# A gate-and-up feed-forward block: all weights of F tiles 0 to 3 are loaded before the transposed x, and eight groups run on 256 tokens first

## The chip, the cores and the metric

The kernel runs on one core of a Trainium2 chip. The metric is the device time of one execution in microseconds, as the median of several runs. Engines are named as in the profile: PE is TensorE (PEld its weight loads), DVE is VectorE, ACT is ScalarE, POOL is GpSimd, SP is SyncE.

## What is computed

```python
B, S, D, F = 1, 2048, 512, 1376        # all bfloat16

def reference(x, w_gate, w_up, w_down):
    g = _silu(x @ w_gate)
    u = x @ w_up
    return (g * u) @ w_down
```

## The kernel before

All of the schedule is written out by hand: each engine has its own list of instructions in program order, and semaphores join the lists. Nothing is reordered by a scheduler.

**Tiles.** Tokens (S = 2048) are cut into four chunks of 512. F = 1376 is cut into ten tiles of 128 and a rest of 96. D = 512 is the contraction of the first two products, in four steps `dk` of 128. A *group* is one PSUM bank: for one chunk and one F tile there is a gate group (G) and an up group (U). Each group is made by four `dk` steps, and each step by two matmuls with 64 weight columns each that run side by side on the two column halves of the array (`gu_step`, L332 to L351). ACT applies silu to the gate bank (L291), DVE multiplies it with the up bank into `hT_sb` (L305). There are eight banks, used in turn; a group may start when the readers of the group eight places before it are done (`free`, L327). Groups of type X and Y do the rest of F. After all four chunks the product with `w_down` follows (L428, L451, L503), and results are copied out and stored.

**Order of groups in a chunk.** G0 U0, G1 U1, then G2 G3 U2 U3, then G4 U4 up to G9 U9, then X (L232).

**The start.** The first matmuls need x transposed (D on partitions). For the first 256 tokens of chunk 0, x is loaded as it lies (`xn_sb`, one load named xn) and transposed on TensorE (L369, L377); DVE and ACT copy the four results to `xT_sb` (L309, L291). All other tokens come by transposing loads: x0b (tokens 256 to 383), x0c (384 to 511), and x1, x2, x3 (512 tokens each). Before xn has landed, TensorE runs matmuls on constants: `N_WARM` of width 512 and `N_FILL` of width 128 (L357 to L362).

**The loads.** Weights of gate and up come in four slabs of F tiles, 0 to 1, 2 to 3, 4 to 6 and 7 to 10, each slab as one gate load (wg0, wg2, wg4, wg7) and one up load (wu0, wu2, wu4, wu7); the last 32 columns of `w_up` have a load of their own (wut), which only the X groups need. ACT issues wg0 (L111); SyncE issues everything else in this order: xn, wu0, x0b, x0c, wg2, wu2, wg4, wu4, wg7, wu7, wut, x1, x2, x3, then the `w_down` loads (L113 to L132). Each load has its own semaphore; `need(name)` makes TensorE wait for it once.

**The first groups.** As only 256 tokens of chunk 0 are there at first, G0, G1, U0 and U1 run on those first (G0 and G1 alternating over `dk`), and then on the other 256 tokens, with G0's first piece cut in two, so that x0b and x0c are waited for one after the other:

```python
            g0, u0, g1, u1 = groups[NT:NT + 4]
            for dk in range(KD):
                for g in (g0, g1):
                    gu_step(g, dk, 0, HT)
            for g in (u0, u1):
                gu_matmuls(g, 0, HT)
            gu_matmuls(g0, HT, HT + P)
            gu_matmuls(g0, HT + P, SC)
            for g in (u0, g1, u1):
                gu_matmuls(g, HT, SC)
```

(HT is 256, P 128, SC 512.) All other groups, from G2 on, run on 512 tokens at once.

Of the kernel before, what the change touches and what calls it, by code (L numbers as in the profile page):

```python
# [6 lines left out]
BF16 = mybir.dt.bfloat16  # L7
FP32 = mybir.dt.float32

N_WARM = 6  # L10
N_FILL = 2


def bass_standalone__swiglu_ffn__prompt_kernel(nc, x, w_gate, w_up, w_down, out):
    _, S, D = x.shape
    F = w_gate.shape[1]
    P = 128
# [13 lines left out]
    HC = P // 2  # L31
    NXN = HT // P
    NB = 8
# [8 lines left out]
    UPH = F + 32  # L42
# [4 lines left out]
    with ExitStack() as es:  # L47
# [19 lines left out]
        banks = [psum[:, i, :] for i in range(NB)]  # L67
# [15 lines left out]
        def load_sem(name):  # L83
            loads[name] = sem(f"s_{name}")
            return loads[name]

        ones_w = nc.const_aps.tensor(1.0, [P, P], BF16)
        ones_m = nc.const_aps.tensor(1.0, [P, SC], BF16)
# [3 lines left out]
        def load_x(eng, name, t0, t1):  # L92
            eng.dma_start_transpose(
                xT_sb[:, :, t0:t1], xf[t0:t1, :]
            ).then_inc(load_sem(name), 16)

        def load_w(eng, name, src, base, f0, f1):
            eng.dma_start(
                w_sb[:, :, base + f0:base + f1],
                src[:, f0:f1].rearrange("(k p) f -> p k f", p=P),  # L100
            ).then_inc(load_sem(name), 16)

        slabs = [(0, 2), (2, 4), (4, 7), (7, NFT)]
        slab_of = {ft: a for a, b in slabs for ft in range(a, b)}

        def load_slab(eng, a, b):
            load_w(eng, f"wg{a}", w_gate, 0, a * P, min(b * P, F))
            load_w(eng, f"wu{a}", w_up, UPH, a * P, min(b * P, F - 32))

        def loads_on_scalar(act):  # L110
            load_w(act, "wg0", w_gate, 0, 0, slabs[0][1] * P)  # L111

        def loads_on_sync(sp):  # L113
            sp.dma_start(
                xn_sb[:, :, :].rearrange("p j d -> p (j d)"), xf[0:HT, :].rearrange("(p j) d -> p (j d)", j=NXN)
            ).then_inc(load_sem("xn"), 16)
            load_w(sp, "wu0", w_up, UPH, 0, slabs[0][1] * P)
            load_x(sp, "x0b", HT, HT + P)
            load_x(sp, "x0c", HT + P, SC)
            for a, b in slabs[1:]:  # L120
                load_slab(sp, a, b)
            load_w(sp, "wut", w_up, F - (F - 32), F - 32, F)
            for c in range(1, NSC):
                load_x(sp, f"x{c}", c * SC, (c + 1) * SC)
            sp.dma_start(
                wd_sb[:, 0:NFF, :], w_down[0:NFF * P, :].rearrange("(k p) d -> p k d", p=P)
            ).then_inc(load_sem("wd"), 16)
            for c in range(NSC):
                sp.dma_start(
                    wdt_sb[R * c:R * (c + 1), :, :], w_down[NFF * P:F, :].rearrange("(q p) d -> p q d", p=R)  # L130
                ).then_inc(load_sem(f"wdt{c}"), 16)
            sp.dma_start(wdl_sb[:, :], w_down[NFF * P:F, LASTA:D]).then_inc(load_sem("wdl"), 16)  # L132
# [3 lines left out]
        groups = []  # L136
# [3 lines left out]
        def add_group(kind, **what):  # L140
            g = dict(kind=kind, at=len(groups), bank=banks[turn[(len(groups) - KD) % NB]], readers=[], **what)
            groups.append(g)
            return g
# [75 lines left out]
        for dk in range(KD):  # L219
            g = add_group("T", dk=dk)  # L220
# [8 lines left out]
        NT = len(groups)  # L229
# [11 lines left out]
        for at in range(NST):  # L241
# [4 lines left out]
            for c0, c1 in [(0, LASTA), (LASTA, LASTB), (LASTB, D)] if end else [(0, D)]:  # L246
                g = add_group("O", t=t, c0=c0, c1=c1, c=c)
# [3 lines left out]
                    eng, g, kind="copy", out=o_sb[ob][:, c0:c1], src=g["bank"][:, 0:c1 - c0],  # L251
# [6 lines left out]
        def rows_of(t):  # L258
            if t < NXN:
                return of[0:HT, :].rearrange("(p j) d -> j p d", j=NXN)[t]  # L260
            return of[t * P:(t + 1) * P, :]
# [14 lines left out]
            ).then_inc(s_I, 1)  # L276

        def on_scalar(act):
            loads_on_scalar(act)
            act.activation(adummy[:, 0:4], zero_c, ACT.Silu)  # L280
            for op in act_ops:
                act.wait_ge(s_P, op["g"]["at"] + 1)
                if op["kind"] == "silu":
                    if op["free"]:
                        act.wait_ge(s_D, op["free"])
                    fn = ACT.Silu
                else:
                    if op["stored"][1]:
                        act.wait_ge(*op["stored"])
                    fn = ACT.Copy  # L290
                act.activation(op["out"], op["src"], fn).then_inc(s_A, 1)  # L291
            for t, c0, c1, ob, eng, n in stores:
                if (c0, c1) == (0, LASTA):
                    act.wait_ge(s_A, n)
                    act.dma_start(rows_of(t)[:, c0:c1], o_sb[ob][:, c0:c1]).then_inc(s_out[ob], 16)
# [16 lines left out]
        def on_tensor(pe):  # L312
# [14 lines left out]
            def free(g):  # L327
                if g["at"] >= NT + NB:
                    for eng, n in groups[g["at"] - NB]["readers"]:
                        after(eng, n)  # L330

            def gu_step(g, dk, n0, n1):  # L332
                c, ft = g["c"], g["ft"]
                if c > 0:
                    need(f"x{c}")
                if c == 0 and n1 > HT:
                    need("x0b")
                if c == 0 and n1 > HT + P:
                    need("x0c")
                if c == 0 and n0 < HT:  # L340
                    after(*xt_ready[dk])
                need(("wg" if g["kind"] == "G" else "wu") + str(slab_of[ft]))
                col = (0 if g["kind"] == "G" else UPH) + ft * P
                for m in (0, HC):
                    ins = pe.matmul(  # L345
                        g["bank"][m:m + HC, n0:n1], lhsT=w_sb[:, dk, col + m:col + m + HC],
                        rhs=xT_sb[:, dk, c * SC + n0:c * SC + n1], start=(dk == 0), stop=(dk == KD - 1),
                        tile_position=(0, m),
                    )
                if n1 == SC and dk == KD - 1:  # L350
                    ins.then_inc(s_P, 1)  # L351

            def gu_matmuls(g, n0, n1):
                for dk in range(KD):
                    gu_step(g, dk, n0, n1)

            def warm(n, width):  # L357
                for i in range(n):
                    pe.matmul(banks[NB - 1][:, 0:width], lhsT=ones_w, rhs=ones_m[:, 0:width], start=True, stop=True)  # L359

            warm(N_WARM, SC)
            warm(N_FILL, P)  # L362
            pe.wait_ge(s_J, 1)
            need("xn")
            for dk in range(KD - 1):
# [11 lines left out]
                    ins = pe.transpose(tview_last()[m:m + HC, i, :], xn_sb[:, i, c0:c0 + HC], ident[:, :])  # L377
            ins.then_inc(s_P, 1)

            g0, u0, g1, u1 = groups[NT:NT + 4]  # L380
            for dk in range(KD):
                for g in (g0, g1):
                    gu_step(g, dk, 0, HT)
            for g in (u0, u1):
                gu_matmuls(g, 0, HT)
            gu_matmuls(g0, HT, HT + P)
            gu_matmuls(g0, HT + P, SC)
            for g in (u0, g1, u1):
                gu_matmuls(g, HT, SC)

            for g in groups[NT + 4:]:
                kind = g["kind"]
                if kind == "O":
                    break
                free(g)
                if kind in "GU":
                    gu_matmuls(g, 0, SC)
                elif kind == "X":
                    c = g["c"]
                    need(f"wg{slab_of[NFF]}")  # L400
                    need("wut")
                    for dk in range(KD):
                        for m in (0, HC):
                            ins = pe.matmul(  # L404
                                g["bank"][m:m + HC, :], lhsT=w_sb[:, dk, XC0 + m:XC0 + m + HC],
                                rhs=xT_sb[:, dk, c * SC:(c + 1) * SC],
                                start=(dk == 0), stop=(dk == KD - 1), tile_position=(0, m),
                            )
                    ins.then_inc(s_P, 1)
                elif kind == "Y":  # L410
                    need(f"wu{slab_of[NFF]}")
                    for dk in range(KD):
                        for c in (2 * g["pi"], 2 * g["pi"] + 1):
                            y0, y1 = yblk(c)
                            ins = pe.matmul(  # L415
                                g["bank"][y0:y1, :], lhsT=w_sb[:, dk, YC0:YC0 + 64],
                                rhs=xT_sb[:, dk, c * SC:(c + 1) * SC],
                                start=(dk == 0), stop=(dk == KD - 1),
                                tile_position=(0, y0), skip_group_check=True,
                            )  # L420
                    ins.then_inc(s_P, 1)
# [78 lines left out]
            for g in last:  # L500
# [4 lines left out]
                    start=False, stop=True, skip_group_check=True,  # L505
# [35 lines left out]
```

## Time and profile before

| | us |
|---|---|
| median of 3 runs | 119.92 (119.9 to 120.52) |
| span of the profiled execution | 118.3 |
| median minus that span | 1.62 |
| PE busy in the span | 115.6 |
| DVE busy | 43.4 |
| ACT busy | 35.5 |
| first matmul on constants | 0.77 |
| first transpose on TensorE | 3.77 |
| first matmul of a group | 4.51 |
| first matmul of an X group (end of chunk 0's other groups) | 21.82 |

For the profiled execution the span is the only time that is given; the runs of the median are other executions. Times within an execution are counted from the start of the span. Busy time of PE counts matmuls from start to a modelled end, and neighbours overlap, so that the spacing of starts tells more than the mean duration does. The time of a DMA issue is the time it holds the issuing engine's queue; its landing is counted from the start of the issue. "Wait" in the text means that an engine stands still for a semaphore.

### The profile page before, as it was taken

The page shows a single profiled execution, that of the slowest core. Times are in us where ns is not written, and L with a number is a line of the kernel's source. Part 1 is how long each engine was busy: PE and PEld are TensorE (multiplying, and loading weights), DVE is VectorE, ACT ScalarE, POOL GpSimd, SP SyncE. Part 2 cuts the span into 40 slices and gives each one's busy share as a digit, 9 for nine tenths or more (in the row PEclk, how much of TensorE's full clock was granted, in tenths as well). Part 3 has the DMA queues.
Part 4 walks back from the last instruction along what each step waited for, and adds up shares of the span by engine and source line. Part 5 has one row for each costly group of instructions (what it writes and reads, how often), then busy time and mean ns, then how long its engine had stood idle before and what let it go on. Part 6 is the DMA issues. An engine that isn't in the chain of part 4 may idle for free.

```text
span 118.3 us, 2985 instructions
## 1 busy us (share of the span) xinstructions
PE 115.6 (98%) x1342; PEld 69.8 (59%) x1342; DVE 43.4 (37%) x68; ACT 35.5 (30%) x61; POOL 0.4 (0%) x5
## 2 busy tenths in 40 slices
PE   7999999999999999999999999999999999999993
PEld 2786666666666666666666666654444444464452
DVE  0133443353433443524442534369700040214331
ACT  5244324454234364243264232370000030203001
POOL 1000000000000000000000000000000000000000
DMA  3999999990000000000000000000000032050512
GB/s 90 272 287 345 225 224 247 309 241 19 0 6 0 0 0 6 0 0 6 0 6 0 0 0 0 6 0 0 6 0 6 0 105 78 0 178 32 195 44 89
DMA packets 16540, 8.92 MB, mean 75 GB/s; under 512 B 8592, under 2 KB 16400, under 8 KB 16528
## 3 DMA queue, kind: packets, MB, share of 16 engines
q1 hardware_dynamic: 15856, 8.38, 27.3%
q10 hardware_dynamic: 672, 0.36, 1.0%
q8 instruction: 10, 0.16, 0.6%
q14 instruction: 2, 0.02, 0.0%
HBM read 4.81 MB, written 2.10 MB: 58 GB/s over the span
## 4 chain that ended last, share of the span: by engine, by line
PE 98%; DVE 0%; issue 0%
PE psum L345 59%; PE psum L451 24%; PE psum L428 7%; PE psum L404 3%; PE psum L359 2%; PE psum L415 1%; PE psum L369 0%; PE psum L377 0%; DVE o_sb L309 0%; PE psum L503 0%
## 5 line engine op out<-in xcount | busy, mean ns | idle before, releaser
L345 PE MATMUL psum<-xT_sb,w_sb 128*64 128x512 bf16 (+2 forms) x680 | 69.9, 367 | 0.0
L345 PEld LDWEIGHTS psum<-xT_sb,w_sb 128*64 128x64 bf16 x680 | 46.0, 110 | 23.0
L305 DVE TENSOR_TENSOR hT_sb<-sg_sb,psum 128x512 bf16<-128x512 f32 x40 | 27.5, 688 | 40.4 <-PE psum L345 36.6
L291 ACT ACTIVATE sg_sb<-psum 128x512 f32<-128x512 f32 x40 | 23.8, 596 | 40.5 <-PE psum L345 40.5
L451 PE MATMUL psum<-wd_sb,hT_sb 32*128 32x512 bf16 x480 | 26.9, 374 | 0.0
L451 PEld LDWEIGHTS psum<-wd_sb,hT_sb 32*128 32x128 bf16 x480 | 13.0, 93 | 13.0 <-issue 0.4
L309 DVE CAST o_sb<-psum 128x512 bf16<-128x512 f32 (+1 forms) x11 | 6.4, 603 | 25.2 <-PE psum L451 19.9
L291 ACT ACTIVATE o_sb<-psum 128x512 bf16<-128x512 f32 (+1 forms) x7 | 3.7, 580 | 33.0 <-PE psum L451 25.9
L428 PE MATMUL psum<-wd_sb,hT_sb 128*128 128x512 bf16 (+2 forms) x60 | 8.9, 308 | 0.0
L428 PEld LDWEIGHTS psum<-wd_sb,hT_sb 128*128 128x128 bf16 x60 | 4.6, 98 | 4.6 <-issue 0.4
L305 DVE TENSOR_TENSOR ht_sb<-sgy_sb,yu_sb 32x512 bf16<-32x512 f32 x8 | 5.5, 683 | 0.4
L404 PE MATMUL psum<-xT_sb,w_sb 128*64 128x512 bf16 x32 | 4.2, 379 | 0.0
L305 DVE TENSOR_TENSOR ht_sb<-sgx_sb,psum 32x512 bf16<-32x512 f32 x4 | 2.8, 692 | 3.5 <-ACT sgx_sb L291 3.5
L291 ACT ACTIVATE sgx_sb<-psum 32x512 f32<-32x512 f32 x4 | 2.3, 587 | 4.5 <-PE psum L404 4.5
L359 PE MATMUL psum<-const-bfloat16-1.0 128*128 128x512 bf16 (+1 forms) x8 | 2.9, 545 | 0.8 <-PEq L526 0.8
L451 PE MATMUL psum<-wdt_sb,ht_sb 32*128 32x512 bf16 (+1 forms) x48 | 3.3, 371 | 0.0
L404 PEld LDWEIGHTS psum<-xT_sb,w_sb 128*64 128x64 bf16 x32 | 2.2, 110 | 1.2
L359 PEld LDWEIGHTS psum<-const-bfloat16-1.0 128*128 128x128 bf16 x8 | 1.0, 136 | 2.4 <-issue 2.4
L291 ACT ACTIVATE sgy_sb<-psum 64x512 f32<-64x512 f32 x4 | 2.4, 589 | 0.1
L451 PEld LDWEIGHTS psum<-wdt_sb,ht_sb 32*128 32x128 bf16 x48 | 1.3, 93 | 1.3
L415 PE MATMUL psum<-xT_sb,w_sb 128*64 128x512 bf16 x16 | 1.9, 379 | 0.0
L280 ACT ACT_TABLE_LOAD x1 | 1.3, 1283 | 1.2 <-PEq L526 1.2
(19 smaller groups left out, 7.2 us busy)
## 6 DMA issues: line engine op xcount, KB each, us to landing
out_dram<-o_sb SPq DMA_DIRECT2D x15, 128.0 KB, 1.8
wd_sb<-in_w_down_dram SPq DMA_DIRECT2D x1, 1280.0 KB, 8.0
w_sb<-in_w_up_dram SPq DMA_DIRECT2D x2, 256.0 KB, 3.9
w_sb<-in_w_gate_dram SPq DMA_DIRECT2D x1, 480.0 KB, 6.7
w_sb<-in_w_up_dram SPq DMA_DIRECT2D x1, 448.0 KB, 7.3
w_sb<-in_w_gate_dram SPq DMA_DIRECT2D x1, 384.0 KB, 4.9
w_sb<-in_w_up_dram SPq DMA_DIRECT2D x1, 384.0 KB, 5.9
wdt_sb<-in_w_down_dram SPq DMA_DIRECT2D x4, 96.0 KB, 6.3
```

Source lines behind the costliest of these rows:

```text
L280: act.activation(adummy[:, 0:4], zero_c, ACT.Silu)
L291: act.activation(op["out"], op["src"], fn).then_inc(s_A, 1)
L305: ins = dve.tensor_tensor(op["out"], op["a"], op["b"], ALU.mult)
L309: ins = dve.tensor_copy(op["out"], op["src"])
L345: ins = pe.matmul(g["bank"][m:m + HC, n0:n1], lhsT=w_sb[:, dk, col + m:col + m + HC], rhs=xT_sb[:, dk, c * SC + n0:c * SC + n1], start=(dk ...
L359: pe.matmul(banks[NB - 1][:, 0:width], lhsT=ones_w, rhs=ones_m[:, 0:width], start=True, stop=True)
L404: ins = pe.matmul(g["bank"][m:m + HC, :], lhsT=w_sb[:, dk, XC0 + m:XC0 + m + HC], rhs=xT_sb[:, dk, c * SC:(c + 1) * SC], start=(dk == 0), ...
L415: ins = pe.matmul(g["bank"][y0:y1, :], lhsT=w_sb[:, dk, YC0:YC0 + 64], rhs=xT_sb[:, dk, c * SC:(c + 1) * SC], start=(dk == 0), stop=(dk == ...
L428: ins = pe.matmul(g["bank"][:, 0:c1 - c0], lhsT=hT_sb[:, fk, t * P:(t + 1) * P], rhs=wd_sb[:, fk, c0:c1], start=(start and fk == 0), stop= ...
L451: ins = pe.matmul(g["bank"][:, 0:c1 - c0], lhsT=h(r, g["t"]), rhs=w[R * r:R * (r + 1), c0:c1], start=(start and n == 0), stop=final, tile_ ...
```

## The change

The warm-up has five matmuls of width 512 rather than six, and the fill behind it is four pairs of matmuls of 64 rows each, one in each row half of the array and each into a bank of its own, rather than two matmuls of 128 rows. ACT issues no load any more. SyncE issues xn, wg0, wu0, wg2, wu2, wut, x0b, x0c, wg4, wu4, wg7, wu7, x1 and so on. TensorE runs the first eight groups (G0 and G1 alternating, U0, U1, G2, G3, U2, U3) on tokens 0 to 255, then G0 on tokens 256 to 383 and 384 to 511, then the other seven on tokens 256 to 511; groups from G4 on run on 512 tokens.

```diff
-N_WARM = 6
-N_FILL = 2
+N_WARM = 5
+N_FILL = 4
...
-        def loads_on_scalar(act):
-            load_w(act, "wg0", w_gate, 0, 0, slabs[0][1] * P)
-
         def loads_on_sync(sp):
             sp.dma_start(
                 xn_sb[:, :, :].rearrange("p j d -> p (j d)"), xf[0:HT, :].rearrange("(p j) d -> p (j d)", j=NXN)
             ).then_inc(load_sem("xn"), 16)
-            load_w(sp, "wu0", w_up, UPH, 0, slabs[0][1] * P)
+            for a, b in slabs[:2]:
+                load_slab(sp, a, b)
+            load_w(sp, "wut", w_up, F - (F - 32), F - 32, F)
             load_x(sp, "x0b", HT, HT + P)
             load_x(sp, "x0c", HT + P, SC)
-            for a, b in slabs[1:]:
+            for a, b in slabs[2:]:
                 load_slab(sp, a, b)
-            load_w(sp, "wut", w_up, F - (F - 32), F - 32, F)
...
         def on_scalar(act):
-            loads_on_scalar(act)
             act.activation(adummy[:, 0:4], zero_c, ACT.Silu)
...
             warm(N_WARM, SC)
-            warm(N_FILL, P)
+            for i in range(N_FILL):
+                for h in range(2):
+                    pe.matmul(
+                        banks[NB - 2 + h][:, 0:P], lhsT=ones_w[h * HC:(h + 1) * HC, :],
+                        rhs=ones_m[h * HC:(h + 1) * HC, 0:P], start=True, stop=True, tile_position=(h * HC, 0),
+                    )
...
-            g0, u0, g1, u1 = groups[NT:NT + 4]
+            first = groups[NT:NT + NB]
+            g0, u0, g1, u1 = first[:4]
             for dk in range(KD):
                 for g in (g0, g1):
                     gu_step(g, dk, 0, HT)
-            for g in (u0, u1):
+            for g in [u0, u1] + first[4:]:
                 gu_matmuls(g, 0, HT)
             gu_matmuls(g0, HT, HT + P)
             gu_matmuls(g0, HT + P, SC)
-            for g in (u0, g1, u1):
+            for g in first[1:]:
                 gu_matmuls(g, HT, SC)
 
-            for g in groups[NT + 4:]:
+            for g in groups[NT + NB:]:
```

## The prediction

> **What bounds the kernel now.** I read the page first, then the chain of work that ended last in order of time, then the start of the kernel in finer steps. The page:
>
> ```profile
> span 118.3 us, 2985 instructions
> PE 115.6 (98%) x1342; PEld 69.8 (59%) x1342; DVE 43.4 (37%) x68; ACT 35.5 (30%) x61; POOL 0.4 (0%) x5
> PE 98%; DVE 0%; issue 0%
> ```
>
> TensorE is the chain. What the chain does at the start is seen in its first pieces (start, length, what):
>
> ```profile
> 0.77 2.93 PE psum L359 x8
> 3.71 0.06 issue
> 3.77 0.51 PE psum L369 x12
> 4.27 0.31 PE psum L377 x3
> 4.58 17.44 PE psum L345 x200
> ...
> 22.88 17.27 PE psum L345 x160
> ```
>
> A full chunk of 512 tokens takes 17.27 us for 80 pairs of 64-column matmuls, 216 ns a pair. The first chunk runs from 4.51 to 21.82 us, 17.31 us, though it is cut into smaller pieces and its data arrives while it runs. So it loses at most 0.04 us, and only two things can change the time: when the first real matmul starts (4.51), and whether a load comes later than TensorE needs it. The loads are issued by SyncE thus (start, time on its queue):
>
> ```profile
> 0.74 0.40 SPq L114 DMA_DIRECT2D xn_sb<-in_x_dram  x1
> 1.20 0.41 SPq L98 DMA_DIRECT2D w_sb<-in_w_up_dram  x1
> 1.66 2.58 SPq L93 DMA_TRANSPOSE xT_sb<-in_x_dram  x2
> 4.29 0.58 SPq L98 DMA_DIRECT2D w_sb<-in_w_gate_dram  x1
> 4.92 0.50 SPq L98 DMA_DIRECT2D w_sb<-in_w_up_dram  x1
> ...
> 8.83 10.05 SPq L93 DMA_TRANSPOSE xT_sb<-in_x_dram  x3
> ```
>
> and, asked for narrow windows, the list of DMA issues gives the time to landing (last number):
>
> ```profile
> xn_sb<-in_x_dram SPq DMA_DIRECT2D x1, 256.0 KB, 2.9
> w_sb<-in_w_gate_dram ACTq DMA_DIRECT2D x1, 256.0 KB, 3.6
> w_sb<-in_w_up_dram SPq DMA_DIRECT2D x1, 256.0 KB, 4.0
> xT_sb<-in_x_dram SPq DMA_TRANSPOSE x1, 4.1
> xT_sb<-in_x_dram SPq DMA_TRANSPOSE x1, 3.2
> ```
>
> Adding issue and landing: xn 3.64, wg0 (issued on ACT at 0.75) 4.35, wu0 5.20, x0b 5.77, x0c (issued 2.98) about 6.2. Needed: xn at once, wg0 by 4.51, wu0 by 5.39, x0b by 6.26, x0c by 6.48. So x0c arrives 0.26 us early and everything is just in time. From 2.7 to 5.5 us the DMA engines are full (share 1.05 to 1.32 in the windows table); at 5.5 to 6.0 they fall to 0.73 and 89 GB/s, because SyncE spent 1.66 to 4.25 on the two transposing loads.
>
> **The change, part by part.** All times on the scale of the span.
>
> 1. Start. xn keeps its place and issue time. Its sixteen completion increments come in two halves, at 3.07 to 3.19 and at 3.45 to 3.64; the late half still has packets of about 245 ns, against 84 ns undisturbed, when wg0's first packets appear at 2.73 on engines that have finished xn. If that disturbance vanished altogether xn would land by 3.19, 0.45 earlier; if it stays, nothing changes. In the changed kernel wg0 stands behind xn in the same queue, issued at 1.20; wg2 on a drained queue took from 4.29 to 5.53, 1.24 us, to its first packet, so wg0 has packets ready at 2.44 and goes on at the same 2.73. So most of the disturbance stays: I take 0.15 earlier. The fill no longer stands in the way: five 512-wide warm-ups at 427 ns and four pairs of 107 ns end at 0.77 + 2.13 + 0.43 = 3.33 (now 3.51). If the row halves did not run as pairs it would be 3.76, a cost of about 0.1; but the transposes of L369 show pairs, two of them every 53 ns at the same cold clock.
>
> 2. wg0 from ACT to SyncE. Issue moves by 0.45 later, but each DMA engine drains xn, then wg0, then wu0 in one row (32 packets of 512 B at 27 ns, 0.86 us each load), so landing at 4.35 and 5.20 stays. Taken as 0; if the cover at 2.73 were gone it is 0.45 late. ACT loses an issue of 0.46 us ahead of a table load that ends at 2.53, long before its first copy at 4.20: 0. The Trainium skill, "DMA: Bandwidth & Descriptors", section "Issuing engines are not separate DMA queues", says that DMAs from different engines share the same 16 DMA engines and that spreading them saves only issue time. By that rule the 0.15 of step 1 would be nothing too, and the sum 0.15 larger; the packets, which drain one load after another on each engine, agree.
>
> 3. x0b and x0c move behind wg2, wu2 and wut: three loads ahead of two, on full engines. One 256 KB load behind another costs 0.85 us in the stream (wu0 behind wg0) and up to 1.13 (wg2 lands at 7.49, wu2 at 8.62). I take the first for wg2, the second for wu2: 6.05 and 7.18. wut has 32 packets of 64 B an engine at 11 ns: 0.35, so 7.53. x0b came 0.57 behind wu0 and x0c 0.45 behind x0b: 8.10 and 8.55. TensorE needs them later than before: four more half groups, each four pairs of 109 ns (0.436 us), so wg2 is due at 4.51 + 4 x 0.436 = 6.26, wu2 at 7.13, x0b at 8.00 and x0c 0.22 later, 8.22. Lateness: wg2 none, wu2 0.05, x0b 0.10, x0c 0.33. These don't add; the latest decides, so 0.35, with 0.05 by the short interval throughout (8.27) and 0.6 by the long one. What waits behind it is all of TensorE, which runs in order; ACT and VectorE have nothing to give there.
>
> 4. Smaller pieces: 16 full pairs become 32 half pairs, 32 x 109 - 16 x 216 = 0.03 us.
>
> 5. The loads behind. SyncE reaches wg4 at about 6.2 to 6.6, not 5.46 (five weight issues of 0.46 to 0.55 ahead of two transposing ones of 1.27), while the engines are still at x0b and x0c, so the dip at 5.5 to 6.0 goes. wg4 landed at 10.36 and wu4 at 11.91 and are due at 11.47 and 12.33; behind x0c at 8.55 they come one and two 384 KB loads later (1.55 between them now): 10.1 and 11.65. Cost 0, and at most 0.3 if that cover went. x1 lands at 17.0 and is due at 22.7, with over five to spare; wut is not due before 21.8. All banks are free again in time: silu 0.60 and multiply 0.69 for each gate and up pair of 0.87.
>
> Sum: -0.15 + 0.35 + 0.03 = +0.23. The profiled execution would have a span of about 118.5. The median of the runs shown is 119.92, 1.62 above the span; I carry that over unchanged: 120.2 (119.6 to 120.6 from the ends of steps 1 and 3).
>
> **The rivals.**
>
> Faster. xn lands with its first half, at 3.19: transposes start 0.4 earlier, the late half of the engines catches up, and x0c is on time. That gives -0.37, 119.55. For more, the thin covers have to count: 0.26 at x0c, 0.42 at wu4. The three runs spread over 0.62 us, which may be such waits in executions other than the profiled one; the new order removes them for wg4 and wu4. Together down to -0.9, 119.0. For it: two halves of xn's landing, and the dip at 5.5. Against: the profile shows no wait to be removed after 4.51.
>
> Slower, by a full queue. x1's issue took 5.60 us against 2.38 and 1.99 for the same load twice later; it was over at 14.43, when wu7 landed (7.11 + 7.3 = 14.4). With five weight loads outstanding the issue waits. In the changed kernel x0b is issued at about 3.6 behind wg0, wu0, wg2, wu2 and wut, also five, and x0c, wg4 and wu4 are queued behind it on SyncE. If x0b has to wait for wu0 or wg2 (5.2, 6.05), x0c's issue ends at about 7.3 to 8.2, and lands some 1.8 after, as x0c now does against its end of issue at 4.25 (6.2) with a little queue in that: 9.1 to 9.9. Late by 0.9 to 1.7, less 0.15: 120.7 to 121.5. It decides from the point where the issue of x0b takes over 2 us. Against: x0b has a quarter of x1's packets, and may fit where x1 did not.
>
> Slower, by the clock. 512-wide warm-ups are 427 ns apart, the same width later 216; the last cold spacing is at 4.32 and the first fast one at 4.51, about 3.6 us after TensorE's first matmul, so real work starts just as the clock does. The new fill ends 0.18 earlier and leaves a longer gap before the transposes. If the change of clock then came one such stretch later, 3.6 us would run at half speed: 1.8 lost, 121.7. Against: more gap is little, and the granted clock is 1.00 throughout. The Trainium skill, "TensorE: Matmul & The Clock Gate", Part 1, has such a gate with a free-running window of 3.4 us; the 3.6 us here agrees, and one trace can't show whether the window is free-running.
>
> No effect: xn and every load as now, x0c within its 8.22: +0.03, 119.95.
>
> **How the numbers follow.** A measurement of this kernel can tell about 0.5%, 0.6 us, from no change: below 119.3 counts as faster, above 120.5 as slower. Forecast 0.34, of which 0.08 above 120.5; faster rival 0.28, 0.24 of it below 119.3; queue 0.24; clock 0.06; no effect 0.08. Faster 0.24; same 0.26 + 0.04 + 0.08 = 0.38; slower 0.08 + 0.24 + 0.06 = 0.38. The range leaves out the clock (0.06), the far end of the queue (0.07) and that of the faster rival (0.04): 119.1 to 121.1. The forecast's own range is 119.6 to 120.6.
>
> **What would show it.** Step 1: start of the first transpose (3.77 now) at about 3.6; at 3.4 the faster rival. Step 2: landing of wg0 at 4.3 and wu0 at 5.2. Step 3: a gap or a longer spacing in TensorE near 8.0 to 8.6, and x0c landing at 8.3 to 8.8. Queue: SyncE's time for x0b over 2 us. Clock: 256-wide pairs of the first groups 214 ns apart instead of 109. Step 5: no wait at 11 to 13 us, and 17.27 us for each later chunk. If TensorE has no gap in the first chunk and starts as now, or the gap exceeds 1 us, my landing times are wrong.

## The result and the profile after

The changed kernel is slower: 121.25 us (median of 7, 120.77 to 122.63) against 120.12 us before (median of 7 in the same comparison), a ratio of 1.0103 with a 95% interval of 1.0075 to 1.0132. That is 0.15 outside the range that I gave (119.1 to 121.1), and on the side of the queue rival (120.7 to 121.5), not of the forecast (120.2). The ratios here and below leave out executions more than 1.5% slower than the fastest of the same kernel; the medians hold them all. The profiled execution took 122.63 us, the longest of the seven, so it shows more than the usual loss; the profile of old_fill below, a kernel with the same loads (120.91 us), is nearer to the median.

The page of the changed kernel, the lines that answer to those of before (span, engines, and the chain by engine):

```profile
span 121.2 us, 3058 instructions
PE 117.7 (97%) x1378; PEld 72.2 (60%) x1379; DVE 43.4 (36%) x68; ACT 35.4 (29%) x61; POOL 0.4 (0%) x5
PE 87%; SPq 6%; DMA 5%; issue 1%; DVE 0%
```

Before, TensorE alone was the chain (98%). Now the first 14 us of it belong to SyncE's queue and to one DMA. In order of time (start, length, what):

```profile
3.91 2.68 SPq L93
...
6.63 1.26 SPq L93
...
7.94 6.10 DMA w_sb<-in_w_gate_dram
14.04 0.14 issue
14.17 1.06 PE psum L342 x8
...
25.79 17.27 PE psum L342 x160
```

SyncE stands 2.68 us in the issue of x0b, then 1.26 in that of x0c, reaches wg4 only at 7.94 (before: 5.46), wg4 lands 6.10 later, and TensorE's first 512-wide group (G4) starts at 14.17. Before, it started at 11.47. That is 2.70 of the 2.9 us between the two spans; the wait for wu4 behind it is 0.2. Each later chunk again takes 17.27.

The chain names what came last; it does not say what the wait cost. TensorE's own lines do (in brackets the idle time before the line):

```profile
4.75 9.02 PE L342 MATMUL psum<-xT_sb,w_sb 128*64 128x256 bf16 x136
14.17 1.06 PE L342 MATMUL psum<-xT_sb,w_sb 128*64 128x512 bf16 x8 [0.41 <-DMA w_sb<-in_w_gate_dram]
```

The last pair ahead of G4 started at 13.49, so with wg4 there G4 would have started at 13.60. By this spacing TensorE stood still for 0.57 us at wg4, and for 0.17 more at wu4. The other 2.13 us of G4's delay were lost earlier in this execution: the first group started at 4.75 instead of 4.51, wu0 (landed at 6.57) cost about 0.16, and 16 pairs ran 213 ns apart instead of 109, which is about 1.7. In old_fill and no_wait_x0 below, the stops at wg4 and wu4 together come to 0.72 and 0.52 us. Before, there is no such stop. So in these three profiles the late wg4 and wu4 cost 0.5 to 0.7 us, where the medians of the same kernels lie 0.7 to 1.1 us above the kernel before.

The DMA engines in the meantime (last two columns: their share and GB/s):

```profile
7.00:8.00 1.00, 1.00 (x14) 0.85 (x12) 0.00 (x0) 0.00 (x0) 0.00 (x0) 1.00 1.00 84
8.00:9.00 1.00, 1.00 (x18) 0.94 (x16) 0.00 (x0) 0.00 (x0) 0.00 (x0) 1.00 0.85 146
9.00:10.00 1.00, 1.00 (x24) 1.00 (x22) 0.00 (x0) 0.00 (x0) 0.00 (x0) 1.00 0.59 65
```

Before they moved 294, 309 and 347 GB/s in these three microseconds. The dip that I had expected to close has become longer: no load is queued behind x0c until SyncE has issued wg4.

### The profile page after: what moved, and what is told of

Read it like the earlier page. It is cut to its first block, busy times and chain, and to the rows that moved or that the text cites. A ratio compares the mean times of both kernels' runs of the same rounds, so it can differ in the third digit from the quotient of the medians.

```text
span 121.2 us, 3058 instructions
## 1 busy us (share of the span) xinstructions
PE 117.7 (97%) x1378; PEld 72.2 (60%) x1379; DVE 43.4 (36%) x68; ACT 35.4 (29%) x61; POOL 0.4 (0%) x5
## 4 chain that ended last, share of the span: by engine, by line
PE 87%; SPq 6%; DMA 5%; issue 1%; DVE 0%
PE psum L342 52%; PE psum L454 24%; PE psum L431 7%; DMA w_sb<-in_w_gate_dram 5%; SPq L93 3%; PE psum L407 3%; SPq L98 2%; PE psum L418 1%; SPq L111 0%; DVE o_sb L306 0%; PE psum L506 0%
## 5 line engine op out<-in xcount | busy, mean ns | idle before, releaser
L342 PE MATMUL psum<-xT_sb,w_sb 128*64 128x512 bf16 (+2 forms) x712 | 72.1, 364 | 0.5 <-DMA w_sb<-in_w_gate_dram 0.4
L342 PEld LDWEIGHTS psum<-xT_sb,w_sb 128*64 128x64 bf16 x712 | 48.5, 113 | 23.4 <-ACT sg_sb L288 0.6
L306 DVE CAST o_sb<-psum 128x512 bf16<-128x512 f32 (+1 forms) x11 | 6.4, 604 | 25.2 <-PE psum L454 19.9
L356 PE MATMUL psum<-const-bfloat16-1.0 128*128 128x512 bf16 x5 | 2.3, 621 | 0.8 <-PEq L529 0.8
L407 PEld LDWEIGHTS psum<-xT_sb,w_sb 128*64 128x64 bf16 x32 | 2.3, 110 | 1.2
L306 DVE COPY xT_sb<-psum 128x256 bf16<-128x256 bf16 x2 | 0.5, 292 | 2.8 <-PE psum L371 2.8
```

The lines of the kernel that those rows point to most:

```text
L306: ins = dve.tensor_copy(op["out"], op["src"])
L342: ins = pe.matmul(g["bank"][m:m + HC, n0:n1], lhsT=w_sb[:, dk, col + m:col + m + HC], rhs=xT_sb[:, dk, c * SC + n0:c * SC + n1], start=(dk ...
L407: ins = pe.matmul(g["bank"][m:m + HC, :], lhsT=w_sb[:, dk, XC0 + m:XC0 + m + HC], rhs=xT_sb[:, dk, c * SC:(c + 1) * SC], start=(dk == 0), ...
```

## The experiments

Three theories. **W**: x0b holds SyncE, wg4 is issued late, and TensorE waits for wg4. **X**: TensorE waits for x0b and x0c (the place where prediction and queue rival had it). **Clock**: the new fill makes TensorE's clock switch later. For Clock there is something in the profile: the 256-wide pairs were 213 ns apart until 8.4 us and 109 after, while before they were 109 apart from 4.5 on. Below, the wider spacing is called half pace.

**again**: the changed kernel as it is.

> The changed kernel once more, for a second profile. Queue theory (the issue of x0b waits until loads ahead of it have landed, so x0c lands near 9.5 and TensorE waits from about 8.0): 256-wide pairs 109 ns apart from 4.5 us on, one wait of 0.9 to 1.3 us ahead of x0b and x0c, about 121.2 us. Clock theory (the shorter fill makes the clock switch one stretch later): pairs 213 ns apart until about 8.4, no wait for x0b or x0c, about 121.2 to 122.6 us. In both, SyncE's time for x0b is about 2.7 us.

121.01 us against 120.19 (23 runs of the kernel before), ratio 1.0062 (1.0033 to 1.0091). So the loss is 0.6 to 1.0%. The execution that was profiled here took 248.7 us with TensorE at half its pace from end to end, and I read no stage of TensorE from it. On SyncE's queue x0b took 1.50 us, not the 2.7 that both theories expected; wg4 was issued at 6.70 and landed at 10.45.

**old_fill**

```diff
-N_WARM = 5
-N_FILL = 4
+N_WARM = 6
+N_FILL = 2
...
-            for i in range(N_FILL):
-                for h in range(2):
-                    pe.matmul(
...
+            warm(N_FILL, P)
```

> The changed kernel with the fill of the kernel before (six warm-ups of 512, two of 128 rows by 128). Queue theory: no effect, 121.2 us and the same wait at 8 to 9.5. Clock theory: the clock switches at 4.4 in the profile and the time goes back to about 120.1.

121.18 us, 1.0096 (1.0064 to 1.0128): the old fill brings nothing back. Its chain of waits:

```profile
3.86 1.62 SPq L93
5.52 1.26 SPq L93
6.83 5.63 DMA w_sb<-in_w_gate_dram
12.60 10.71 PE psum L342 x96
```

The same links with a shorter hold: G4 starts at 12.60, 1.13 later than before, and the span is 1.3 longer (119.6). Of the 1.13, TensorE stood still for 0.59 at wg4 (and for 0.13 more at wu4 behind it); the rest is pairs at half pace until 5.7. It did not stand still at x0b or x0c in this execution.

**new_fill_alone**: the kernel before with the new fill.

> The kernel before with only the fill of the changed one (five warm-ups, four pairs of 64 rows). Queue theory: same as before within 0.3 us, 120.1. Clock theory: slower by about 1.1 us or more, with 256-wide pairs 213 ns apart in the profile.

119.97 us, 0.9984 (0.9952 to 1.0016). With old_fill this closes the Clock theory: neither fill changes the time by an amount that could be measured.

**x0_early**

```diff
-            for a, b in slabs[:2]:
-                load_slab(sp, a, b)
-            load_w(sp, "wut", w_up, F - (F - 32), F - 32, F)
+            load_slab(sp, *slabs[0])
             load_x(sp, "x0b", HT, HT + P)
             load_x(sp, "x0c", HT + P, SC)
+            load_slab(sp, *slabs[1])
+            load_w(sp, "wut", w_up, F - (F - 32), F - 32, F)
```

> The changed kernel with x0b and x0c issued right behind wu0, ahead of wg2, wu2 and wut; wg0 stays on SyncE, the eight groups and the new fill stay. Queue theory: SyncE's time for x0b is 1.3 us, x0b and x0c land before 6.8, no wait for them at 8.0; 120.0 to 120.3 us. Clock theory: no effect, 121.2 us.

121.72 us, 1.013 (1.0093 to 1.0168): both expectations missed. x0b is no longer held (the two issues take 2.58 together) and x0c lands at 6.27, but I had not moved the due times: with eight groups first, wg2 is needed at 6.26 (6.77 in this execution, with its half pace until 5.6), and it now stands behind the two transposing issues and lands at 8.16. The timeline of TensorE, with the idle time in brackets:

```profile
4.52 2.42 PE L342 MATMUL psum<-xT_sb,w_sb 128*64 128x256 bf16 x32
8.20 1.06 PE L342 MATMUL psum<-xT_sb,w_sb 128*64 128x256 bf16 x16 [1.27 <-DMA w_sb<-in_w_gate_dram]
```

It doesn't tell W from X. It shows that two transposing issues cost whatever weight load stands behind them about 2.6 us of issue time, here (2.58) as in the kernel before (2.58).

**no_wait_x0**: the waits for x0b and x0c taken out of the first eight groups, whose second half now reads the x of tokens 0 to 255.

```diff
-                if c == 0 and n1 > HT:
-                    need("x0b")
-                if c == 0 and n1 > HT + P:
-                    need("x0c")
+                r0 = n0 - HT if c == 0 and n0 >= HT else n0
+                if c == 0 and n0 == 0 and n1 > HT:
+                    need("x0b")
+                    need("x0c")
...
-                        rhs=xT_sb[:, dk, c * SC + n0:c * SC + n1], start=(dk == 0), stop=(dk == KD - 1),
+                        rhs=xT_sb[:, dk, c * SC + r0:c * SC + r0 + n1 - n0], start=(dk == 0), stop=(dk == KD - 1),
```

> The changed kernel, but the split pieces of chunk 0 (tokens 256 to 511 of the first eight groups) read the x of tokens 0 to 255, so that nothing waits for x0b and x0c there; both loads are still issued as before. Theory W (x0b holds SyncE, wg4 is issued late and TensorE waits for wg4 at F tile 4): no change, 121.0 to 121.3 us, and the profile shows TensorE standing still at the first 512-wide group. Theory X (TensorE waits for x0b and x0c): back to 120.0 to 120.3. If both waits lie one behind the other, one alone gives little.

120.81 us, 1.0059 (1.0026 to 1.0092). Still slower than before by about as much as the changed kernel (the interval meets both of its own). The chain again goes through the hold to wg4:

```profile
3.97 2.39 SPq L93
...
7.72 5.07 DMA w_sb<-in_w_gate_dram
...
12.92 1.42 PE psum L342 x9
```

In this execution TensorE also waited for wu0, which landed at 6.35. The list of waits has it (us in total, times, longest):

```profile
PE psum L342 <- DMA w_sb<-in_w_up_dram: 0.9, 1, 0.9
```

By the spacing of the starts this stop was 1.08 us, longer than the one at wg4 (0.37).

**no_wait_wg4**: the waits for wg4 and wu4 taken out of chunk 0, whose F tiles 4 to 6 now use the weights of tiles 1 to 3.

```diff
+                if c == 0 and 4 <= ft < 7:
+                    ft -= 3
                 need(("wg" if g["kind"] == "G" else "wu") + str(slab_of[ft]))
```

> The changed kernel, but in chunk 0 the F tiles 4 to 6 use the weights of tiles 1 to 3, so that nothing waits for wg4 and wu4 before chunk 1; the loads are issued as before. Theory W: back to 120.0 to 120.3 us. Theory X: no change, 121.0 to 121.3, with a gap ahead of the first 128-wide pieces.

120.23 us against 120.07, 1.0011 (0.9979 to 1.0042). This is W: with this wait gone nothing measurable is left of the loss, although x0b is held as long as ever (2.49) and x0c lands at 9.26. X has no share of its own that could be measured. The profiled execution is the slowest of the ten (120.75): its chain goes through wu0, which landed at 6.36 and stopped TensorE for 0.54 us. So a late wu0 can cost something in a single execution, but it does not show in the median.

**late_wg4_alone**: the converse, one line in the kernel before.

```diff
-            for a, b in slabs[1:]:
-                load_slab(sp, a, b)
+            load_slab(sp, *slabs[1])
+            sp.wait_ge(loads["wg2"], 16)
+            for a, b in slabs[2:]:
+                load_slab(sp, a, b)
```

> The kernel before with one line more: SyncE waits for wg2 (landed at 7.5) before it issues wg4, so that wg4's issue moves from 5.5 to about 7.5, where the changed kernel has it; everything else, the order of loads and the four groups too, stays. Theory W (the late issue of wg4 is what costs): wg4 lands at 11.1 to 12.5 against 11.47 when it is needed, and TensorE stands still there; 120.5 to 121.2 us. If something else in the change costs: same as before within 0.2.

120.94 us against 119.75, 1.0079 (1.005 to 1.0107): a late wg4, together with wu4 and what else is queued behind it, gives the loss of the whole change. Its profile has wg4's issue on SyncE's queue at 7.44:

```profile
7.44 0.37 SPq L98 DMA_DIRECT2D w_sb<-in_w_gate_dram  x1
```

and by the list of DMA issues it takes 4.1 us to land, at 11.5, when G4 is due at 11.47:

```profile
w_sb<-in_w_gate_dram SPq DMA_DIRECT2D x1, 384.0 KB, 4.1
```

In that one execution (span 118.8, the fastest of its seven) TensorE does not stand still at G4: its half pace lasted until 5.7, which put G4 back to 11.99. The stop itself is seen in after, old_fill and no_wait_x0; for late_wg4_alone only the time says it.

**wut_late**

```diff
-            load_w(sp, "wut", w_up, F - (F - 32), F - 32, F)
             load_x(sp, "x0b", HT, HT + P)
             load_x(sp, "x0c", HT + P, SC)
             for a, b in slabs[2:]:
                 load_slab(sp, a, b)
+            load_w(sp, "wut", w_up, F - (F - 32), F - 32, F)
```

> The changed kernel with wut issued behind wu7, so that one load fewer lies ahead of x0b and x0c. Theory W: SyncE's time for x0b falls from 1.6 to 2.7 us to about 1.3, wg4 is issued at about 6.0 instead of 6.7 to 7.9; 120.4 to 120.8 us. Theory X: x0c lands 0.35 earlier, 120.8 to 120.9. If neither the hold nor the order counts: 121.2.

120.57 us, 1.0038 (1.0005 to 1.007). This lies below both results of the changed kernel (1.0062 and 1.0103), as W had it, but its interval overlaps that of again (1.0033 to 1.0091), so how much of the loss is gone can't be told. The hold did not fall to 1.3: x0b's issue took 2.08, but it began at 3.31, and wg4 went out at 6.74 and landed at 10.63. TensorE does not stop at wg4 in this execution, whose span is 1.1 longer than before; the half pace until 6.7 accounts for about that.

**room_in_queue**: wut late, and wg0 on ACT as before.

```diff
-            for a, b in slabs[:2]:
-                load_slab(sp, a, b)
-            load_w(sp, "wut", w_up, F - (F - 32), F - 32, F)
+            load_w(sp, "wu0", w_up, UPH, 0, slabs[0][1] * P)
+            load_slab(sp, *slabs[1])
             load_x(sp, "x0b", HT, HT + P)
             load_x(sp, "x0c", HT + P, SC)
             for a, b in slabs[2:]:
                 load_slab(sp, a, b)
+            load_w(sp, "wut", w_up, F - (F - 32), F - 32, F)
...
+            load_w(act, "wg0", w_gate, 0, 0, slabs[0][1] * P)
             act.activation(adummy[:, 0:4], zero_c, ACT.Silu)
```

> The changed kernel with two loads less ahead of x0b on SyncE: wg0 is issued by ACT as in the kernel before, and wut goes behind wu7; order of the other loads, eight groups and fill stay. Theory W: x0b is no longer held on SyncE (1.3 us instead of 1.5 to 2.7), wg4 is issued at about 5.4; 119.7 to 120.2 us, at least as fast as before. If the hold comes from something other than the number of loads ahead in SyncE's queue: 120.6 or more, x0b still over 2 us.

120.05 us against 119.75, 1.0012 (0.999 to 1.0033): as fast as before, with weights first and eight groups first. SyncE's queue:

```profile
2.76 2.97 SPq L93 DMA_TRANSPOSE xT_sb<-in_x_dram  x2
5.78 0.58 SPq L98 DMA_DIRECT2D w_sb<-in_w_gate_dram  x1
```

wg4 is issued at 5.78 and lands 3.7 later, at 9.5, two microseconds ahead of its need. Not all of the expectation came true: the first of the two transposing issues, x0b, still took 1.66 instead of 1.3. wg4 is issued 2.16 earlier than in the profile after: 1.15 of it because x0b's issue starts at 2.76 instead of 3.91, 1.02 because it takes less time. The kernel doesn't beat the one before; nothing tried here does.

**x0_on_act**: x0b and x0c issued by ACT.

```diff
-            load_x(sp, "x0b", HT, HT + P)
-            load_x(sp, "x0c", HT + P, SC)
...
             for a, b in slabs[2:]:
                 load_slab(sp, a, b)
+            sp.wait_ge(load_sem("x0b"), 16)
+            sp.wait_ge(load_sem("x0c"), 16)
...
-            for op in act_ops:
+            for n, op in enumerate(act_ops):
+                if n == 2:
+                    load_x(act, "x0b", HT, HT + P)
+                    load_x(act, "x0c", HT + P, SC)
```

> The changed kernel with x0b and x0c issued by ACT, behind its two copies of transposed x (at about 5.1 us), and SyncE going straight on to wg4, wu4, wg7, wu7; SyncE waits for x0b and x0c before x1. Theory W: wg4 is issued at 3.9 and lands by 10; 119.8 to 120.2 us. Theory X: x0b and x0c share the engines with wg4 and land near 9; 121.2 or more.

127.61 us, 1.0526 (1.0399 to 1.0653). W's expectation is missed by 7 us, and X's sign is right with a size that I hadn't seen: wg4 is issued at 3.85 and lands at 8.83, but x0c takes 8.2 us to land beside SyncE's loads, and TensorE has to wait for it until 13.99:

```profile
5.76 8.19 DMA xT_sb<-in_x_dram
```

The two stops (3.25 us at x0b, 1.75 at x0c) are not all of it: behind them the granted clock was 0.50 from 14.4 to 19.9, with pairs 213 ns apart, about 2.8 us more.

**four_groups**

```diff
-            first = groups[NT:NT + NB]
+            first = groups[NT:NT + 4]
...
-            for g in [u0, u1] + first[4:]:
+            for g in (u0, u1):
...
-            for g in first[1:]:
+            for g in (u0, g1, u1):
...
-            for g in groups[NT + NB:]:
+            for g in groups[NT + 4:]:
```

> The changed kernel with only four groups run first on 256 tokens, as before; loads and fill stay. TensorE then needs x0b at about 6.3 instead of 8.0, and x0b lands at 7.8 to 8.9 in the runs so far: 1.5 to 2.5 us of waiting, of which the later wait for wg4 no longer takes anything, since four more half groups are left to do behind it. Theory W and theory X both: 121.8 to 123. If x0b's landing does not matter at all: 121.2.

122.4 us, 1.0202 (1.0166 to 1.0239), as expected. Here TensorE stands still for 1.66 us at x0b and 0.29 at x0c, which ends the wait (5.32 + 3.03 in the chain, then TensorE at 8.39). So the eight groups are worth about 1.0 to 1.4% under the new order of loads (1.0202 against 1.0103 and 1.0062); they do what they are there for, and it is the load behind x0c that isn't covered.

## Why the prediction was wrong

The step that failed is step 5, "Cost 0, and at most 0.3 if that cover went". It had two wrong sizes.

*Issue of wg4.* I let SyncE issue two transposing loads at 1.27 each and came to 6.2 to 6.6. Measured: 7.94, 6.83 (old_fill), 7.72 (no_wait_x0), 7.73 (no_wait_wg4), but 6.70 and 6.63 in again and four_groups, which have the same order of loads. The issue of x0b took 2.68, 1.62, 2.39, 2.49, 1.50 and 1.42 there, and it ended when wu0 had landed: 6.58 against 6.57 in the profile after, 5.48 against 5.39, 6.36 against 6.35, 6.37 against 6.36, 5.35 against 5.26 and 5.28 against 5.21. The landing of wu0 in the profile after is its issue at 1.66 plus

```profile
w_sb<-in_w_up_dram SPq DMA_DIRECT2D x1, 256.0 KB, 4.9
```

This is the mechanism of the queue rival, whose deciding point (over 2 us) the profile after passes; old_fill stays below it (1.62) and is slower by as much, so that point doesn't separate a loss from none. I gave the rival 0.24, and I had its next link wrong: I priced the hold at x0c, while the same hold moves wg4, which was even named there as queued behind x0b. That its time, 120.7 to 121.5, holds the measured 121.25 is luck. Step 5 worked wg4 out with the undisturbed issue times only.

*Landing of wg4.* I had 10.1, one 384 KB load behind x0c. Measured: 14.04, 12.46 (old_fill), 12.78 (no_wait_x0), 12.47 (no_wait_wg4), and 10.45 and 10.21 in again and four_groups, near the forecast. With these loads ahead of it, it takes 3.6 to 6.1 us from its issue, and its sixteen increments (a load's semaphore is counted up in sixteen steps) don't always come together: in the profile after fifteen are there by 11.72 and the last at 14.04; in old_fill fourteen by 10.43, the fifteenth at 10.73 and the last at 12.46. Before, the same tail (9.68 and 10.34) lay under 1.1 us of cover. How much of the usual loss belongs to the late issue and how much to the tail, one profile of each kernel can't tell; that the late issue is enough for it, late_wg4_alone shows.

The other steps. Step 1: the first transpose was at 3.80 instead of 3.6 in the profile after, and the first group started at 4.75; but it started at 4.40 to 4.47 in old_fill, no_wait_x0, no_wait_wg4 and wut_late against 4.51: 0.04 to 0.11 earlier, a little less than the 0.15 I took. Step 2: wg0 landed at 4.26 to 4.33 in these, as forecast; wu0 at 5.39, 6.36, 6.36 and 6.11, not 5.20, since the last of its increments were late, and this feeds the hold. Step 3: x0c landed at 8.35 to 9.49 with this order of loads, around or beyond my 8.55, and it still isn't what costs: where G4 waits for wg4 anyway, an earlier wait takes nothing more, and with wg4's wait gone 1.0011 is left. Step 4 holds.

The clock rival was right in what the profile after looks like (213 ns until 8.4), and in that one execution the half pace is most of the loss. It was wrong as the effect of the new fill, and as the cause of the usual loss, since without wg4's wait a ratio of 1.0011 is left. Counting matmuls between 4.75 and 6.25 us, the profile before has 32 and the profile after 16:

```profile
4.75:6.25 1.50, 1.50 (x32) 1.00 1.03 176
```

```profile
4.75:6.25 1.50, 1.50 (x16) 1.00 1.07 313
```

But the half pace was over when the first group started in no_wait_x0 and four_groups (4.4) and in room_in_queue (4.5), and ended at 5.7 in old_fill and late_wg4_alone, at 6.7 in wut_late, at 8.4 in the profile after: old and new fill on both sides. The Trainium skill, "TensorE: Matmul & The Clock Gate", Part 1, has a free-running window of 3.4 us, so that the switch depends on where in it a kernel starts. That the switch moves from one execution to the next agrees with the traces here; their spread, at least 4.0 us, is wider than that window.

The rule that I cited on issuing engines came out true and was of little use: by "DMA: Bandwidth & Descriptors" of the Trainium skill, section "Issuing engines are not separate DMA queues", moving wg0 to SyncE costs only issue time, "which is usually small relative to the DMA itself". The landing of wg0 agrees: 4.26 to 4.33 in the four profiles above, 4.38 before. Issue time was lost here, 0.15 to 1.4 us of it in x0b alone against the 1.27 of an undisturbed issue, and room_in_queue gets the time back by taking two loads from ahead of x0b.

## What to carry to other kernels

When a load is moved, follow the issuing queue to the first load *behind* it that something waits for, and price that one with the issue times of a full queue, not with those of a free one. A slack of a microsecond at a load can be used up by the slowest of its sixteen increments alone; look at the last one, not at the usual one. The chain that ended last names a wait, but not its cost: measure how long the engine itself stood still, and what it had lost before. To find which of several late loads costs, let the consumer use data that is there already in place of one of them, and delay that one alone in the kernel before: the two runs together settled here that wg4 and wu4, issued late, are what costs.

## What the runs showed of the hardware that was not expected

The issue of the transposing load x0b ended within 0.1 us of the landing of wu0 in six profiles out of six with the same loads ahead of it; with one load fewer (wut_late) it ended before wu0 landed (5.38 against 6.11), so what is counted is not simply loads, and I have not settled what it is. The sixteen increments of a load right ahead of a transposing one mostly come together (wu0 before: 5.06 to 5.21), while those of other loads spread more (wg0 before: 3.90 to 4.38). Not always: of wut in the profile after, four came at 6.64 to 6.87 and twelve at 8.18 to 8.35. Why is open. A transposing load on ACT's queue beside weight loads on SyncE's took 7.5 and 8.2 us to land, against 2.8 to 5.2 for the same loads on SyncE's own. Why the last increments of a load come 0.5 to 2.3 us behind the others in some executions stays open.
